# A 128x1 memset behind every indirect DMA, gathers four steps ahead, and silu one step later in an edge message-passing kernel

## The chip, the cores and the metric

The kernel runs on one core of a Trainium2 chip. The time is device microseconds for one execution of the program, the median of several runs. A profile is the record of one further execution on the same kind of core: its span goes from the first to the last recorded instruction. The engines are named as in the profile: PE (TensorE), ACT (ScalarE), DVE (VectorE), POOL (GpSimd) and SP (SyncE, which issues DMAs).

## The reference

The reference is one layer of message passing on a graph with N = 12,500 nodes of D = 64 features and E = 800,000 edges with 4 features each; H = 128.

```python
def reference(x, e_attr, src, dst, w1, b1, w2, b2):
    h_src = x[src]
    h_dst = x[dst]
    m_in = concatenate([h_src, h_dst, e_attr], axis=-1)
    h = silu(m_in @ w1 + b1)
    msg = h @ w2 + b2
    return segment_sum(msg, dst, N)
```

Since the sum over edges is linear, the kernel sums the hidden rows h of each node first, with a count of the edges, and multiplies the sums by w2 once per node at the end.

## The kernel before

**Tables.** At the start the products of x with the source part and with the target part of w1 are made for all nodes. The source product goes to the table `Atab` in device memory, one row of 512 bytes a node. The target product stays on chip as `Btab`.

**Sorting.** The edges come in no order. The kernel sorts them by target into 98 buckets of 128 nodes, in 16 portions. For each portion, `rank` counts the edges of each bucket, and `place` (line 879) moves the edges' records to their places: one-hot matmuls (L983) into a PSUM tile `pl`, a copy by ACT into `cb` (L958), and an indirect DMA of GpSimd that scatters the rows of `cb` into a buffer `buf` in device memory (L944). All but the first portion is sorted while edges of earlier portions are already worked on.

**The main loop.** `run` (line 1193) goes over 1590 steps of 512 sorted edges (4 tiles of 128). What step n needs is issued by small functions, each some steps ahead or behind (the constants of line 1187):

- `load` (SP, 11 steps ahead) and `pairs` (SP, 10 ahead) bring the edges' sources and targets, for two steps at once; `sources` (DVE, L1091, 8 ahead) turns them into row numbers `ix`.
- `gather` (GpSimd, 6 ahead) issues four indirect DMAs (L1155), each of 128 rows of `Atab`, into one of seven buffers `ga`.
- `spread` (SP, 4 ahead), `marks` (DVE, 1 ahead) and `targets` (ACT, L1118 and L1119, 2 ahead) prepare the edge features `pts`, the one-hot tiles `ob` of the sums, and the one-hot tiles `oT` of the targets.
- `pre` (PE, step n itself) sums edge features (L1143), target rows (L1145) and the gathered source rows (L1147) in a PSUM tile `px`. L1147 is the last reader of `ga`.
- `silu` (ACT, L1166, step n itself, right after `pre`) writes h from `px`. `onehot` (ACT, L1162) makes `sg` from `ob` one step later.
- `seg` (PE, L1174, two steps later) sums h by node into another tile of the same three PSUM buffers as `px`, and `accum` (DVE, L1182) adds that to the sums `S` in SBUF.

Between these stand pieces of `rank` and `place` for later portions. `filler` deals them out by estimated costs over the steps. Every engine executes its instructions in the order in which the code writes them (`in_order`, line 1047), so a waiting instruction holds up all that is written behind it on its engine. Two waits matter for the gathers: for `ix`, and for a `ga` buffer. With seven buffers and a lead of six, the gathers for step n+6 write the buffer of step n-1, which is free when L1147 of step n-1 is done.

After the loop the sums are transposed, multiplied by w2, and written out.

Of the kernel before, what the change touches and what calls it, by code (L numbers as in the profile page):

```python
# [11 lines left out]
BF = mybir.dt.bfloat16  # L12
# [69 lines left out]
def tile_mpnn(ctx, tc, x, e_attr, src, dst, w1, b1, w2, b2, out, portions):  # L82
# [8 lines left out]
    VE, SC, GP, PE = nc.vector, nc.scalar, nc.gpsimd, nc.tensor  # L91
# [728 lines left out]
    def records(p, c0, cn):  # L820
# [53 lines left out]
        p["rec", c0] = (pay, lo, hv)  # L874
        yield 1200

    below = [zero[:, :CS * PC], zero[:, :CS * PC]]

    def place(p):
# [20 lines left out]
        for c0 in range(0, cols, PW):  # L900
# [6 lines left out]
            for g in range(c0 // GT, -(-(c0 + cn) // GT)):  # L907
# [10 lines left out]
                for s0 in range(0, gt, SUB):  # L918
                    flush(pend, 1)
                    sn = min(SUB, gt - s0)  # L920
                    co = None
                    if s0 + sn == gt:

                        if s0 < 2 * SUB:
                            flush(pend, 0)
                        co = wk.tile([128, NLO], BF, name="co")
                        VE.tensor_scalar(co[:R], io3[:R], p["cin"][:R, g:g + 1], None, op0=OP.is_equal)
                        yield 229
                    mk = wk.tile([128, SUB, CS * PC], FH, name="mk")
                    VE.tensor_tensor(  # L930
                        mk[:EP, :sn].bitcast(I32).rearrange("p s (f j) -> p s f j", f=PC),
                        half_[:, s0:s0 + sn].unsqueeze(2).to_broadcast([EP, sn, PC, CS // 2]),
                        pay[:EP, go + s0:go + s0 + sn].rearrange("p s w t -> p s (w t)").bitcast(I32).unsqueeze(3)
                        .to_broadcast([EP, sn, PC, CS // 2]), op=OP.bitwise_and)
                    yield 430
                    oh = wk.tile([128, SUB, NLO], BF, name="oh")
                    VE.tensor_tensor(  # L937
                        oh[:EP, :sn].rearrange("p s (j t) -> p s j t", t=2),
                        io3[:EP].rearrange("p (j t) -> p j t", t=2).unsqueeze(1).to_broadcast([EP, sn, NLO // 2, 2]),
                        lo[:EP, go + s0:go + s0 + sn].unsqueeze(2).to_broadcast([EP, sn, NLO // 2, 2]), op=OP.is_equal)  # L940
                    yield 700

                    def scatter(ix_, n_, rows_):
                            stn = GP.indirect_dma_start(  # L944
                                out=buf, out_offset=bass.IndirectOffsetOnAxis(ap=ix_, axis=0),
                                in_=rows_, in_offset=None, bounds_check=NCH - 1, oob_is_err=False)
                            tc.add_to_no_dep_group(f"S{k}", stn.ins)
                            for kk in range(k + 1):
                                tc.declare_no_dep(stn.ins, group=f"S{kk}", reason="distinct rows")
                            for kk in range(k + 1, len(ports)):  # L950
                                tc.declare_no_dep(stn.ins, group=f"Z{kk}", reason="rows of later portions alone")
                            if k:
                                tc.declare_no_dep(stn.ins, group="L", reason="rows of an earlier portion")

                    def store(g, pa):
                        flush(scat, 2)
                        cb = wk.tile([128, NQ + 1, CS * PC], FH, name="cb", bufs=3)
                        SC.activation(cb.rearrange("p q c -> p (q c)"), pa, AF.Copy)  # L958
                        below[:] = cb[:, 1], cb[:, 2]
                        todo = [(p["idx"][:, g:g + 1], 128, cb[:, 0])]  # L960
                        if g + 1 == ngr:
                            todo.append((p["idx"][:, ngr:ngr + 1], 128, cb[:, 1]))
                            if k == last:
                                todo.append((p["fidx"][:R, 0:1], R, cb[:R, 2]))
                        for i, a in enumerate(todo):
                            defer(scat, lambda a=a: scatter(*a), 3 + i)


                    d, at = (1, 0) if clock["half"] else (0, 3)

                    def mm(g=g, s0=s0, mk=mk, oh=oh, gt=gt, sn=sn, co=co, at=at):
                        if s0 == 0:
                            box[0] = ps.tile([128, (NQ + 1) * CS * PC], F32, name="pl", bufs=2)
                        pa = box[0]
                        done_ = s0 + sn == gt
                        terms = [(oh[:EP, i], mk[:EP, i])
                                 for i in range(sn)]
                        if done_:
                            flush(evac, 0)
                            terms.append((co[:R], below[1][:R]))  # L980
                        for i, (oh_, mv) in enumerate(terms):
                            for u in range(3):
                                PE.matmul(pa[:, u * CS * PC:(u + 1) * CS * PC], oh_[:, u * 128:(u + 1) * 128], mv,  # L983
                                          start=s0 + i + u == 0, stop=False)
                        if done_:
                            PE.matmul(pa[:, :CS * PC], idb, below[0], start=False, stop=True)
                            defer(evac, lambda: store(g, pa), int(at == 3), 3 - at)
                    defer(pend, mm, d, at)
                    yield 229
                    subs -= 1  # L990
                    while nxt is not None:
                        c = next(nxt, None)
                        if c is None:
                            nxt = None
                            break
                        yield c
                        if subs > 0:
                            break
# [152 lines left out]
    def gather(n):  # L1151
        s = st[n]
        ga = wk.tile([128, 4, 2 * H], FH, name="ga", bufs=NGA)
        for t in range(4):
            GP.indirect_dma_start(out=ga[:, t, :], out_offset=None, in_=Atab,  # L1155
                                  in_offset=bass.IndirectOffsetOnAxis(ap=s["ix"][:, t:t + 1], axis=0))
        s["ga"] = ga

    def onehot(n):
# [24 lines left out]
            st.pop(n)  # L1184
            bts.pop(n)

    LL, LP, LX, LG, LS, LR, LT = 11, 10, 8, 6, 4, 1, 2
    phase = []
    for k, b in enumerate(sure):
        assert b > len(phase) + LL + 2  # L1190
# [2 lines left out]
    def run(m0, m1, filler):  # L1193

        bt = bt0 = None
        prev = {}
        ahead = m0
        for n in range(m0 - LL, m1 + 2):
            def on(lag):
                return m0 <= n + lag < m1  # L1200
            m = n + LL
            i0 = traced()
            clock["now"] = n
            if on(LL):
                k = phase[m] if m < len(phase) else len(ports) - 1
                filler(m, 0)
                if m % 64 == 0 or m == m0 or m < len(phase) and phase[m - 1] != k:
                    bt, bt0 = bucket_table(k, 2 * m), 2 * m
                bts[m] = (bt, 2 * m - bt0)
                if m == ahead:  # L1210
                    w = min(WL, m1 - m, len(phase) - m if m < len(phase) else WL)
                    w = 1 + sum(all(phase[m + j] == k for j in range(1, i + 1) if m + j < len(phase)) for i in range(1, w))
                    load(m, k, w)
                    ahead += w
            if on(LP):
                pairs(n + LP)
            if on(LX):
                sources(n + LX)
            if on(LG):
                gather(n + LG)  # L1220
            if on(LS):
                spread(n + LS)
            if on(LR):
                marks(n + LR)
            if on(LT):
                targets(n + LT)
            if on(-2):
                seg(n - 2)
            if on(-1):
                onehot(n - 1)  # L1230
            if on(0):
                pre(n)
                silu(n)
            at_place(0, n)
            at_place(1, n)
            for t in range(4):
                clock["half"] = int(t > 1)
                filler(n, 1 + t)
                if t == 1:
                    at_place(2, n)  # L1240
                if on(-2) and t == 3:
                    accum(n - 2, 0)
            filler(n, 5)
            if on(-2):
                accum(n - 2, 1)
            at_place(3, n)
            in_order(i0, prev)
        clock["now"] = None
        assert not any(places)
# [175 lines left out]
```

## Time and profile before

| | |
|---|---|
| median of 3 runs | 11,317.32 us (11,317.08 to 11,324.34) |
| span of the profiled execution | 11,179.7 us |
| instructions recorded | 214,957 |
| mean granted TensorE clock | 0.809 of full speed |
| first gather starts | 317.8 us |
| last gather starts | 11,106.5 us |

The page gives the span of the profiled execution and not its time from outside; the median of the runs lies 137.6 us above the span. Its rows are read thus: a group has line, engine, operation, output and input, shapes and number of instructions, then its busy time, the mean of one in ns, and the idle time of the engine right before these instructions with what ended most of it. "remote" and "issue" stand where no single instruction was found as the one that ended a wait: "issue" is time in which the engine waited for nothing that the profile shows. A row of the timeline has start, duration, engine, line, operation, and in brackets the idle time before it and what ended it.

### The profile page before, as it was taken

How to read it: one execution, taken by the hardware profiler on the slowest of the kernel's cores; microseconds unless marked ns; L12 is line 12 of the kernel's file. 1: busy time of each engine (PE TensorE's matmuls, PEld its weight loads, DVE VectorE, ACT ScalarE, POOL GpSimd, SP SyncE). 2: the span in 40 equal slices, each digit the busy share in tenths (PEclk: the TensorE clock that was granted, in tenths of full speed). 3: DMA queues.
4: the chain of work that ended last, by engine and by line, in shares of the span. 5: the costliest groups of instructions: out<-in, count | busy, mean ns of one | idle time of the engine just before them, and what ended most of it. 6: DMA issues, size and time to landing. Idle time of an engine off the chain costs nothing. (4 is left out here: it accounts for less than half of the span.)

```text
span 11179.7 us, 214957 instructions
## 1 busy us (share of the span) xinstructions
PE 8116.8 (73%) x73739; PEld 6653.7 (60%) x73739; DVE 6365.6 (57%) x18821; ACT 3859.6 (35%) x5331; POOL 6499.4 (58%) x6828
## 2 busy tenths in 40 slices
PE   7677777777777777777777777777777777775556
PEld 5566666666666566566566566666565565554445
DVE  8666676666665555555655555655555665441112
ACT  3233333333333333333333333333333333333333
POOL 1555555555555665566655666566566566666664
PEclk8777888888888778888888888888788887877777
DMA  2334434443443444444444444444444444444444
GB/s 92 64 66 72 67 58 71 65 73 64 72 66 64 76 67 66 76 68 67 77 66 66 76 68 66 74 69 68 75 67 66 74 67 69 69 67 71 72 72 68
DMA packets 3427360, 777.19 MB, mean 70 GB/s; under 512 B 3152950, under 2 KB 3215334, under 8 KB 3425036
## 3 DMA queue, kind: packets, MB, share of 16 engines
q1 hardware_dynamic: 3206638, 316.00, 26.1%
q0 software_dynamic: 218016, 446.07, 15.1%
q8 instruction: 645, 10.57, 0.4%
q14 instruction: 399, 3.27, 0.1%
q10 hardware_dynamic: 1662, 1.29, 0.0%
HBM read 712.51 MB, written 54.08 MB: 69 GB/s over the span
## 5 line engine op out<-in xcount | busy, mean ns | idle before, releaser
L1155 POOL DMA_INDIRECT ga<-Atab,ix x6360 | 6050.6, 951 | 4120.9 <-issue 1511.7
L1166 ACT ACTIVATE h<-px 128x512 f32<-128x512 f32 x1590 | 946.7, 595 | 6596.1 <-remote 2752.7
L1174 PE MATMUL px<-h,sg 128*128 128x129 f32 x12720 | 2375.2, 337 | 928.6 <-issue 387.7
L1174 PEld LDWEIGHTS px<-h,sg 128*128 128x128 f32 x12720 | 2065.8, 240 | 1155.0 <-issue 533.8
L983 PE MATMUL pl<-mk,oh 128*128 128x160 f16 x18750 | 1987.5, 260 | 575.8 <-issue 493.3
L983 PEld LDWEIGHTS <-oh 128*128 128x128 bf16 x18750 | 1637.8, 110 | 1037.3 <-issue 767.7
L1145 PE MATMUL px<-Btab,oT 128*128 x12720 | 1731.0, 249 | 159.4 <-issue 154.0
L1143 PE MATMUL px<-WE,pts 65*128 65x128 bf16 x6360 | 1489.0, 250 | 383.5 <-issue 241.1
L1182 DVE TENSOR_TENSOR S<-S,px 128x129 f32 x3180 | 906.2, 285 | 1341.2 <-remote 562.5
L1145 PEld LDWEIGHTS <-oT 128*128 128x128 bf16 x12720 | 1233.0, 114 | 575.1 <-issue 523.4
L930 DVE TENSOR_TENSOR mk<-fix,pay 128x320 int32<-128x320 int32 x1563 | 758.1, 485 | 1322.5 <-remote 712.0
L937 DVE TENSOR_TENSOR oh<-fix,lo 128x1536 bf16<-128x1536 bf16 x1563 | 1482.4, 948 | 0.1
L1147 PE MATMUL px<-ga,idA 128*128 128x512 f16 x3180 | 1172.0, 454 | 51.6 <-issue 46.2
L591 DVE TENSOR_REDUCE slT<-rx 128x5 f32<-128x490 f32 (+1 forms) x1302 | 833.2, 642 | 614.1 <-remote 305.1
L1119 ACT ACTIVATE oT<-oT,scl 128x1024 bf16<-128x1024 bf16 x795 | 986.1, 1240 | 26.7
L1162 ACT ACTIVATE sg<-ob 128x512 f32<-128x512 bf16 x1590 | 982.1, 618 | 0.0
L1118 ACT ACTIVATE oT<-oT,nip 128x1024 bf16<-128x1024 f16 x795 | 906.9, 1141 | 31.6 <-DMA oT<-dsc 24.7
L1143 PEld LDWEIGHTS <-pts 65*128 65x128 f16 x6360 | 722.2, 114 | 159.6 <-issue 113.1
L583 PEld LDWEIGHTS <-selB 99*128 99x128 bf16 x6250 | 479.1, 108 | 539.7 <-issue 428.3
L1128 DVE TENSOR_TENSOR ob<-fix,d 128x1024 bf16<-128x1024 bf16 x795 | 550.1, 692 | 352.3 <-ACT sg L1162 164.8
L583 PE MATMUL rx<-bT,selB 99*128 99x98 bf16 x6250 | 598.4, 224 | 198.1 <-issue 189.1
L579 PE MATMUL rx<-ohb,triO 128*128 128x490 bf16 (+1 forms) x1302 | 541.6, 416 | 120.5 <-DVE slT L591 49.8
(326 smaller groups left out, 5973.1 us busy)
## 6 DMA issues: line engine op xcount, KB each, us to landing
oT<-dsc SPq DMA_DIRECT2D x795, 256.0 KB
ga<-Atab,ix POOLq DMA_INDIRECT x6360
pts<-buf SPq DMA_DIRECT2D x2385, 16.0 KB
buf<-zero SPq DMA_DIRECT2D x184, 120.0 KB
dsc<-buf SPq DMA_DIRECT2D x795, 4.0 KB
pld<-dsc SPq DMA_DIRECT2D x795, 4.0 KB
Btab<-in_e_attr_dram POOLq DMA_DIRECT2D x10, 1250.0 KB
el<-in_e_attr_dram SPq DMA_DIRECT2D x74, 160.0 KB
```

Source lines behind the costliest of these rows:

```text
L583: PE.matmul(xp[:EP, i * R:(i + 1) * R], selB[:NR, s_:s_ + 1].to_broadcast([NR, EP]), bT[g][:NR, :R], start=False, stop=i == n - 1)
L937: VE.tensor_tensor(oh[:EP, :sn].rearrange("p s (j t) -> p s j t", t=2), io3[:EP].rearrange("p (j t) -> p j t", t=2).unsqueeze(1).to_broadc ...
L983: PE.matmul(pa[:, u * CS * PC:(u + 1) * CS * PC], oh_[:, u * 128:(u + 1) * 128], mv, start=s0 + i + u == 0, stop=False)
L1118: SC.activation(oT, oT.bitcast(FH), AF.Abs, bias=nip1[:, 0:1])
L1119: SC.activation(oT, oT, AF.Relu, scale=scl[:, 2:3], bias=inv)
L1143: PE.matmul(pr[:, sl], s["pts"][:, sl], WE, start=t == 0, stop=False)
L1145: PE.matmul(pr[:, sl], s["oT"][:, sl], Btab[:, ds(v[t // 2], 1), u, :], start=False, stop=False)
L1147: PE.matmul(pr.rearrange("p (t h) -> p t h", t=4), idA, s["ga"][:, :, u * H:(u + 1) * H], start=False, stop=u == 1)
L1155: GP.indirect_dma_start(out=ga[:, t, :], out_offset=None, in_=Atab, in_offset=bass.IndirectOffsetOnAxis(ap=s["ix"][:, t:t + 1], axis=0))
L1162: SC.activation(sg, s["ob"][:, :4].rearrange("p t h -> p (t h)"), AF.Copy)
L1166: SC.activation(hs[n % 3][:, :, :H], st[n]["pr"].rearrange("p (t h) -> p t h", t=4), AF.Silu)
L1174: PE.matmul(s["so"][t // 2], s["sg"][:, t * 128:(t + 1) * 128], hs[n % 3][:, t, :], start=t % 2 == 0, stop=t % 2 == 1)
```

## The change

The change has three parts. GpSimd clears a tile `idle` of 128x1 bf16, which nothing reads, behind each scatter and each gather. The loads, pairs, sources and gathers come two steps nearer to their use, the gathers four steps ahead in place of six; the other leads and the number of `ga` buffers stay. And `silu(n)` is issued early in step n+1, behind the loads and ahead of all else of that step, in place of step n right after `pre(n)`.

```diff
+    idle = cst.tile([128, 1], BF, name="idle")
     below = [zero[:, :CS * PC], zero[:, :CS * PC]]
...
                             stn = GP.indirect_dma_start(
                                 out=buf, out_offset=bass.IndirectOffsetOnAxis(ap=ix_, axis=0),
                                 in_=rows_, in_offset=None, bounds_check=NCH - 1, oob_is_err=False)
+                            GP.memset(idle, 0.0)
...
         for t in range(4):
             GP.indirect_dma_start(out=ga[:, t, :], out_offset=None, in_=Atab,
                                   in_offset=bass.IndirectOffsetOnAxis(ap=s["ix"][:, t:t + 1], axis=0))
+            GP.memset(idle, 0.0)
...
-    LL, LP, LX, LG, LS, LR, LT = 11, 10, 8, 6, 4, 1, 2
+    LL, LP, LX, LG, LS, LR, LT = 9, 8, 6, 4, 4, 1, 2
...
+            if on(-1):
+                silu(n - 1)
             if on(LP):
                 pairs(n + LP)
...
             if on(0):
                 pre(n)
-                silu(n)
             at_place(0, n)
```

Two places show the new order. The first is GpSimd's queue where the second portion's first scatter comes in, behind the gathers of the first thirty steps. Before (the number at the end says how often the row repeats):

```order
L373 MEMSET S 128x1806
L944 DMA buf<-cb,idx 76544x160 x8
L1155 DMA ga<-Atab,ix 128x256 x120
L944 DMA buf<-cb,idx 76544x160
L1155 DMA ga<-Atab,ix 128x256 x12
```

And after, from the last gather ahead of that scatter on (the lines have moved: L1157 is the gather, L945 the scatter, L948 and L1159 the memsets):

```order
L1157 DMA ga<-Atab,ix 128x256
L1159 MEMSET idle 128x1
L945 DMA buf<-cb,idx 76544x160
L948 MEMSET idle 128x1
L1157 DMA ga<-Atab,ix 128x256
L1159 MEMSET idle 128x1
L1157 DMA ga<-Atab,ix 128x256
L1159 MEMSET idle 128x1
```

Gathers and scatters keep their order among each other on this queue; a memset stands behind each.

The second place is ACT's queue in the middle of the loop, in a step that also copies a `pl` tile into `cb`. Before:

```order
L1162 ACTIVATE sg<-ob 128x512
L1166 ACTIVATE h_217<-px 128x4x128
L958 ACTIVATE cb<-pl 128x480
L1162 ACTIVATE sg<-ob 128x512
L1166 ACTIVATE h_219<-px 128x4x128
```

After (L1165 is the copy of `ob`, L960 that of `pl`, L1169 the silu):

```order
L1165 ACTIVATE sg<-ob 128x512
L960 ACTIVATE cb<-pl 128x480
L1169 ACTIVATE h_222<-px 128x4x128
L1165 ACTIVATE sg<-ob 128x512
L1169 ACTIVATE h_218<-px 128x4x128
```

The silu now stands behind the `cb` copy of its step instead of ahead of it; the three h buffers are named by number.

## The prediction

> **What bounds the kernel now.** I read the busy line of the page first, then the stretch from the first gather to the last one, because the share of the span averages a different prologue and epilogue.
>
> ```profile
> PE 8116.8 (73%) x73739; PEld 6653.7 (60%) x73739; DVE 6365.6 (57%) x18821; ACT 3859.6 (35%) x5331; POOL 6499.4 (58%) x6828
> L1155 POOL DMA_INDIRECT ga<-Atab,ix x6360: 942/947/1623, 317.8 to 11106.5; - x199
> 317.50:11108.00 10790.50, 7830.32 (x71293) 6424.31 (x71292) 6072.12 (x17925) 3741.82 (x5126) 6446.50 (x6749) 0.81 0.42 69
> ```
>
> The third row (columns: window, its length, busy time and instructions of PE, PEld, DVE, ACT and POOL, granted clock, DMA share, GB/s) holds the 1590 steps: 10,790.5 us, 6.79 us a step. No engine is full: TensorE 73%, GpSimd 60%. So the bound is a wait, and I ask who waits for whom. GpSimd's groups in that same stretch:
>
> ```profile
> L1155 POOL DMA_INDIRECT ga<-Atab,ix x6360 | 6050.6, 951 | 4120.9 <-issue 1511.7 <-remote 862.2 <-PE px L1147 759.5
> L944 POOL DMA_INDIRECT buf<-cb,idx x388 | 394.9, 1018 | 231.4 <-ACT cb L958 119.8 <-issue 111.0 <-ACT h L1166 0.6
> POOL ga L1155 <- issue: 1511.7, 4896, 4.9
> POOL buf L944 <- issue: 111.6, 366, 0.3
> POOL ga L1155 <- DVE ix L1091: 23.7, 7, 9.4
> ```
>
> It issues 6360 gathers and 389 scatters there. The two issue rows say that 4896 + 366 = 5262 of them start behind another indirect DMA, after a gap of 0.31 us in which nothing is waited for. The timeline shows the pitch, and how one step runs:
>
> ```profile
> 6014.84 0.95 POOL L1155 DMA_INDIRECT ga<-Atab,ix  x1 [1.37 <-remote]
> 6016.09 0.95 POOL L1155 DMA_INDIRECT ga<-Atab,ix  x1 [0.30 <-issue]
> 6016.56 0.59 PE L1147 MATMUL px<-ga,idA 128*128 128x512 f16 x2
> 6017.34 0.94 POOL L1155 DMA_INDIRECT ga<-Atab,ix  x1 [0.30 <-issue]
> 6018.59 0.95 POOL L1155 DMA_INDIRECT ga<-Atab,ix  x1 [0.31 <-issue]
> 6019.84 1.01 POOL L944 DMA_INDIRECT buf<-cb,idx  x1 [0.30 <-issue]
> 6022.04 0.60 ACT L1166 ACTIVATE h<-px 128x512 f32<-128x512 f32 x1 [6.32 <-remote]
> 6022.16 0.49 DVE L930 TENSOR_TENSOR mk<-fix,pay 128x320 int32<-128x320 int32 x1 [1.93 <-remote]
> 6022.27 0.97 POOL L1155 DMA_INDIRECT ga<-Atab,ix  x1 [1.42 <-remote]
> ```
>
> Start to start, a gather takes 1.25 us (6014.84 to 6016.09). Were GpSimd never held up, the stretch would need 6360 x 1.25 + 389 x 1.32 (1.01 + 0.31) = 7950 + 513 = 8463 us. It takes 10,790. The difference, **2327 us or 1.46 us a step**, is what waiting costs.
>
> What does it wait for? The last matmul on the px tile ends at 6017.15. The silu that reads that tile starts at 6022.04, 4.9 us later, and ACT was idle for 6.32 us. In that very moment DVE (6022.16) and GpSimd (6022.27) start as well, all 1.2 to 1.4 us after the last indirect DMA ended (6020.85). The release seems to come with the end of GpSimd's run of DMAs, not with the matmul. The tail, which has no sorting work beside it, shows the same behind a run of eight:
>
> ```profile
> 10400.30 0.95 POOL L1155 DMA_INDIRECT ga<-Atab,ix  x1 [2.09 <-PE px L1145]
> 10406.70 1.06 PE L1147 MATMUL px<-ga,idA 128*128 128x512 f16 x2
> 10409.05 0.94 POOL L1155 DMA_INDIRECT ga<-Atab,ix  x1 [0.30 <-issue]
> 10411.80 0.60 ACT L1166 ACTIVATE h<-px 128x512 f32<-128x512 f32 x1 [7.32 <-PE px L1147]
> 10411.90 0.61 DVE L1182 TENSOR_TENSOR S<-S,px 128x129 f32 x2 [5.33 <-PE px L1147]
> 10412.04 0.95 POOL L1155 DMA_INDIRECT ga<-Atab,ix  x1 [2.04 <-PE px L1147]
> ```
>
> The matmul ends at 10407.76, the silu starts 4.0 us later, 1.8 us behind the end of the run at 10409.99. Now a place where GpSimd had run out of work:
>
> ```profile
> 6032.19 0.95 POOL L1155 DMA_INDIRECT ga<-Atab,ix  x1 [0.30 <-issue]
> 6035.09 1.06 PE L1147 MATMUL px<-ga,idA 128*128 128x512 f16 x2
> 6036.18 0.60 ACT L1166 ACTIVATE h<-px 128x512 f32<-128x512 f32 x1 [6.40 <-PE px L1147]
> 6036.42 0.94 POOL L1155 DMA_INDIRECT ga<-Atab,ix  x1 [3.28 <-PE px L1147]
> ```
>
> GpSimd idle since 6033.14, the matmul ends at 6036.15, the silu starts 0.03 us later. I call it the **hold**: TensorE's progress reaches the others late while a run of indirect DMAs is in the air. GpSimd in turn waits for the buffer that the same step's matmul frees (seven ga buffers, gathers six steps ahead), so hold and buffer chase each other: run, hold, release, run. How the hold comes about the trace doesn't show.
>
> **The change, part by part.** *The memsets.* Behind each of the 6749 indirect DMAs of the stretch stands one more GpSimd instruction. Nothing reads the tile, and it waits for nobody but GpSimd itself. Rows that are near:
>
> ```profile
> 0.27 0.11 POOL L1409 MEMSET const-float32-1.0<- 128x1 f32 x1
> 0.30 0.12 POOL L1409 MEMSET const-bfloat16-1.0<- 128x1 bf16 x1
> 1.43 0.09 POOL L135 MEMSET ones_b<- 128x1 bf16 x1
> 176.87 0.98 POOL L944 DMA_INDIRECT buf<-cb,idx  x1 [3.72 <-ACT cb L958]
> 177.84 0.52 POOL L356 MEMSET sg<- 1x512 f32 x1
> ```
>
> The same tile shape took 0.09 us; two in a row started 0.03 us apart. Behind a scatter a memset started at once (176.87 + 0.98 against 177.84), without the 0.30 us that a DMA behind a DMA shows. Bounds: 0.03 us each when the start-to-start step is what counts, 0.03 x 6749 = 202 us; even a gain is not excluded if the 0.31 us gap shrinks, which I bound at 0.31 x 5262 = 1631 us and think unlikely. From above: 0.09 and a second gap of 0.31, 0.40 x 6749 = 2700 us. I take 0.10 us, by the row of the same shape: **+675 us**.
>
> [...] The memset at 177.84 shows no delay, but it is one. [...]
>
> What the memset does to the hold is the open term. The prologue's lone scatters have a memset behind them, but no matmul that somebody waits for ended in their shadow. From one side it does nothing (the hold hangs on the transfer); from the other it ends it (the hold hangs on GpSimd's program, and an ordinary instruction closes the DMA). The second is nearer to the rows: the waiters start together with the end of the run, however long the run is (five DMAs: 1.2 us after it; eight: 1.8 us), so each DMA that follows another keeps the hold up, and a non-DMA instruction between them breaks just this succession.
>
> *Gathers four steps ahead instead of six.* Seven ga buffers stay. Before, gather n+6 overwrites the buffer of step n-1, which TensorE has only just read; after, gather n+4 takes that of step n-3. The wait for the buffer goes: TensorE may be two steps further behind. What is late next: the data. Issue to use falls from six steps to four, some 24 us at 6 us a step, against a landing that the release rows put at under 2 us; free. load, pairs and sources move with the gather and keep their distance to it; SyncE issues the same DMAs in the same order. On GpSimd's queue gathers and scatters keep their order too, memsets apart.
>
> *silu a step later.* It goes behind the cb copy in some steps:
>
> ```profile
> L958 ACT ACTIVATE cb<-pl 128x480 f16<-128x480 f32 x391 | 221.6, 567 | 457.4 <-remote 264.8 <-PE pl L986 157.3 <-PE px L1147 16.1
> L1166 ACT ACTIVATE h<-px 128x512 f32<-128x512 f32 x1590 | 946.7, 595 | 6596.1 <-remote 2752.7 <-PE px L1147 1959.4 <-PE rx L583 578.0
> ```
>
> The copy need not wait behind a silu whose px is late any more; the silu waits at most one copy, 0.57 us, 391 times. Between 0 and 222 us lost, between 0 and the 120 us that scatters waited for the copy won. Cover: seg, the next reader, comes two steps behind pre, and ACT stands idle 6596 us in front of silus. No PSUM buffer comes free too late: the next to take the px of pre(n) is seg(n), which needs silu(n) anyway. I take 0.
>
> *The sum.* Waits of 2327 us go, except those for data of the step itself, 120 + 24 = 144 us, and half of GpSimd's named waits for L1147 (759.5 / 2 = 380 us), for the places where TensorE really is late, as at 6036.42. Stretch: 8463 + 675 + 144 + 380 = 9662 us. Around it 317.5 us before and 72 after: span 10,051 (before: 11,179.7). The median of the runs is 11,317.32, that is 137.6 us above the span; the same added gives 10,189. I forecast **10,190 us**.
>
> **Rivals.** *B, the hold stays, only the buffer wait goes.* Then GpSimd runs two steps at a stretch, as in the tail: 10400.30 to 10412.04 is 11.74 us for eight gathers, plus scatters 2 x 389/1590 x 1.32 = 0.65, plus 8.5 memsets 0.85: 13.24 per two steps, x 795 = 10,526, + 527 = 11,050 us. For it: the landing, which no memset changes, is what the release follows. Against: it needs the sorting's instructions, of which the tail has none, to fit between.
>
> *C, slower: the hold stays and longer runs starve the rest.* All engines' progress then comes once in two steps, and in the gap behind each run TensorE, ACT and DVE do two steps' dependent work. The tail's gap is 2.04 us; with the sorting's work it would be more, 3.28 us as at 6036.42: (13.24 + 1.24) x 795 + 527 = 12,040 us. It decides from a gap of 2.40 us on, where 13.60 x 795 + 527 = 11,339 passes the time of before.
>
> *D, nothing measurable,* 11,317 us: the memsets vanish in the issue gaps and the hold is as before, one run a step, because something else than the buffer paces GpSimd.
>
> *E, there is no hold.* TensorE's ends in the trace would be early and the silus start when the matmul is really done. Then the buffer wait was no loss by itself, and 5262 back-to-back DMAs grow by 0.10: 11,317 + 526 = 11,843 us. Against it: 0.03 us at 6036.18 and 4.9 us at 6022.04 behind the same line. [...]
>
> **Chances.** The hold ends, 10,190: 0.57 (its own range 9,200, the sum with 0.03 us memsets and no wait left, 8463 + 202 + 527, to 10,860, with 0.20 us memsets). B 0.15, D 0.06, C 0.13, E 0.09. Faster is A and B, 0.72; slower is C and E, 0.22; within 0.2%, about what a measurement of this kernel can tell from no change, D, 0.06. The range reaches from 9,200 to 11,700: below it lies 0.04 of A (memsets that cost less than nothing), above it E and about 0.07 of C, 0.2 together.
>
> **What would show it.** If the hold ends: silus start within 0.1 us of L1147's end while gathers run, ACT's wait before silu turns from remote to the matmul, and GpSimd's gathers follow at 1.3 to 1.4 us with few waits. The memset's price is the start-to-start step of two gathers with it between. If B or C: runs of eight, silus still at a run's end. If E: rows as before with a longer pitch. The forecast fails if the memset opens a second 0.3 us gap, or if TensorE, at 4.9 us of work a step, becomes the bound.

## The result, and the profile after

The changed kernel took 12,639.2 us (median of 4 runs), the kernel before 11,317.2 us on the same chip: **11.6% slower**, ratio 1.1159 with a 95% interval of 1.1143 to 1.1175. The forecast was 10,190 us with a range to 11,700; it had the wrong sign. The outcome is that of rival C, and worse than C was priced.

The page of the changed kernel and its groups (line, engine, operation, tiles, shapes and number; busy us and mean ns of one; idle time before them and what ended it). L1157 is the gather, L1159 the memset behind it, L1169 the silu:

```profile
span 12638.4 us, 222031 instructions
PE 8409.8 (67%) x73739; PEld 6842.4 (54%) x73739; DVE 6357.1 (50%) x18821; ACT 3845.2 (30%) x5331; POOL 7276.7 (58%) x13596
L1157 POOL DMA_INDIRECT ga<-Atab,ix x6360 | 6039.5, 950 | 4732.1 <-issue 2278.4 <-PE px L1177 460.4 <-PE px L1149 460.1
L1159 POOL MEMSET idle<- 128x1 bf16 x6360 | 760.8, 120 | 3.5
L1169 ACT ACTIVATE h<-px 128x512 f32<-128x512 f32 x1590 | 943.6, 593 | 6409.3 <-remote 3401.6 <-PE px L1149 1897.5 <-PE rx L583 387.7
POOL ga L1157 <- issue: 2278.4, 5599, 12.2
```

TensorE, DVE and ACT do the work of before, spread over 1459 us more. The idle time before silus that no single instruction ended grew from 2753 to 3402 us. And 5599 gathers now follow something else on GpSimd with no named wait between, against 4896 before: GpSimd's runs have become longer. Counted over the traces of the loop, where an idle time above 0.6 us ends a run, its indirect DMAs form 1023 runs against 1368, and 563 of them hold eight or nine against 217.

The timeline shows such a run, with GpSimd's DMAs and the other engines' rows around them:

```profile
6039.73 0.94 POOL L1157 DMA_INDIRECT ga<-Atab,ix  x1 [4.78 <-issue]
6040.67 0.12 POOL L1159 MEMSET idle<- 128x1 bf16 x1
6040.98 0.94 POOL L1157 DMA_INDIRECT ga<-Atab,ix  x1 [0.19 <-issue]
6041.98 0.60 ACT L1169 ACTIVATE h<-px 128x512 f32<-128x512 f32 x1 [1.67 <-PE px L1149]
6047.05 0.38 PE L1149 MATMUL px<-ga,idA 128*128 128x512 f16 x1 [0.34 <-issue]
6048.47 0.94 POOL L1157 DMA_INDIRECT ga<-Atab,ix  x1 [0.19 <-issue]
6051.36 0.67 DVE L591 TENSOR_REDUCE slT<-rx 128x5 f32<-128x490 f32 x1 [7.20 <-PE rx L583]
6051.62 0.60 ACT L1169 ACTIVATE h<-px 128x512 f32<-128x512 f32 x1 [8.53 <-PE rx L583]
6055.06 0.94 POOL L1157 DMA_INDIRECT ga<-Atab,ix  x1 [5.53 <-PE px L1177]
```

From 6039.73 to 6049.41 GpSimd sends eight gathers, two steps' worth, at the old pitch of 1.25 us. The memsets sit in the gap between two DMAs: 0.12 us of the 0.31. The matmul on px ends at 6047.43, and its silu starts 4.2 us later, 2.2 us behind the run's end. DVE and ACT have stood for 7.2 and 8.5 us. Only then do they and TensorE do what the next gathers need, and GpSimd waits 5.5 us for it. The windows of this run give the share of each engine (length; busy us and instructions of PE, PEld, DVE, ACT, POOL; clock, DMA share, GB/s):

```profile
6039.70:6044.70 5.00, 4.79 (x55) 4.19 (x53) 4.35 (x14) 1.72 (x4) 4.24 (x8) 0.91 0.41 52
6044.70:6050.70 6.00, 1.97 (x8) 0.72 (x9) 0.00 (x0) 0.00 (x0) 4.24 (x8) 0.73 0.31 55
6050.70:6055.70 5.00, 4.69 (x41) 4.35 (x41) 3.82 (x11) 3.84 (x5) 0.64 (x1) 0.65 0.39 62
```

In the first four gathers the others work off what had been released. In the second four DVE and ACT start no instruction, and TensorE 8 matmuls against 55. The second step's gathers thus run beside engines that do next to nothing, and in the 5 us after them it is GpSimd that idles.

### The profile page after: what moved, and what is told of

It reads as the page before. It is cut to its first block, busy times and chain, and to the rows that moved or that the text cites. A ratio compares the mean times of both kernels' runs of the same rounds, so it can differ in the third digit from the quotient of the medians.

```text
span 12638.4 us, 222031 instructions
## 1 busy us (share of the span) xinstructions
PE 8409.8 (67%) x73739; PEld 6842.4 (54%) x73739; DVE 6357.1 (50%) x18821; ACT 3845.2 (30%) x5331; POOL 7276.7 (58%) x13596
## 5 line engine op out<-in xcount | busy, mean ns | idle before, releaser
L1157 POOL DMA_INDIRECT ga<-Atab,ix x6360 | 6039.5, 950 | 4732.1 <-issue 2278.4
L1177 PE MATMUL px<-h,sg 128*128 128x129 f32 x12720 | 2417.3, 343 | 980.9 <-issue 470.5
L1169 ACT ACTIVATE h<-px 128x512 f32<-128x512 f32 x1590 | 943.6, 593 | 6409.3 <-remote 3401.6
L1177 PEld LDWEIGHTS px<-h,sg 128*128 128x128 f32 x12720 | 2125.5, 247 | 1181.2 <-issue 598.9
L985 PE MATMUL pl<-mk,oh 128*128 128x160 f16 x18750 | 2122.3, 266 | 945.6 <-issue 849.1
L985 PEld LDWEIGHTS <-oh 128*128 128x128 bf16 x18750 | 1693.1, 113 | 1497.5 <-issue 1236.7
L1147 PE MATMUL px<-Btab,oT 128*128 x12720 | 1763.6, 253 | 362.6 <-issue 351.3
L1145 PE MATMUL px<-WE,pts 65*128 65x128 bf16 x6360 | 1514.6, 254 | 728.6 <-ACT h L1169 415.6
L1149 PE MATMUL px<-ga,idA 128*128 128x512 f16 x3180 | 1217.9, 467 | 127.5 <-issue 111.0
L1165 ACT ACTIVATE sg<-ob 128x512 f32<-128x512 bf16 x1590 | 981.7, 617 | 0.0
L960 ACT ACTIVATE cb<-pl 128x480 f16<-128x480 f32 x391 | 221.5, 566 | 2120.3 <-PE pl L988 979.8
L1159 POOL MEMSET idle<- 128x1 bf16 x6360 | 760.8, 120 | 3.5
```

Source lines behind the costliest of these rows:

```text
L1145: PE.matmul(pr[:, sl], s["pts"][:, sl], WE, start=t == 0, stop=False)
L1147: PE.matmul(pr[:, sl], s["oT"][:, sl], Btab[:, ds(v[t // 2], 1), u, :], start=False, stop=False)
L1149: PE.matmul(pr.rearrange("p (t h) -> p t h", t=4), idA, s["ga"][:, :, u * H:(u + 1) * H], start=False, stop=u == 1)
L1165: SC.activation(sg, s["ob"][:, :4].rearrange("p t h -> p (t h)"), AF.Copy)
L1169: SC.activation(hs[n % 3][:, :, :H], st[n]["pr"].rearrange("p (t h) -> p t h", t=4), AF.Silu)
L1177: PE.matmul(s["so"][t // 2], s["sg"][:, t * 128:(t + 1) * 128], hs[n % 3][:, t, :], start=t % 2 == 0, stop=t % 2 == 1)
```

## The experiments

Three theories stood against each other: (1) more free buffers let GpSimd run two steps at a stretch, and the hold then covers both; (2) the memsets lengthen the hold; (3) the silu, now behind a copy that waits for a later matmul, comes too late. Each run was timed beside the kernel before on the same chip; ratios are to that.

### One part at a time

`e1_memset`: the memsets alone.

```diff
+    idle = cst.tile([128, 1], BF, name="idle")
...
                                in_=rows_, in_offset=None, bounds_check=NCH - 1, oob_is_err=False)
+                            GP.memset(idle, 0.0)
...
                                   in_offset=bass.IndirectOffsetOnAxis(ap=s["ix"][:, t:t + 1], axis=0))
+            GP.memset(idle, 0.0)
```

> The memsets alone; leads and silu as before. Theory 1 (runs of eight: the leads free the gathers of the buffer wait, GpSimd sends two steps at a stretch, and TensorE's progress reaches the others once in two steps): runs stay at four or five, and as the changed kernel's gathers still start 1.25 us apart with a memset between, the time stays within 1% of 11,317 us. Theory 2 (the memsets lengthen the hold or break into the release): slower by several per cent, toward 12,600 us, with runs of four and a longer idle time behind each. Theory 3 (the silu behind the copy of pl): 11,317 us as well.

`e2_leads`: the leads alone.

```diff
-    LL, LP, LX, LG, LS, LR, LT = 11, 10, 8, 6, 4, 1, 2
+    LL, LP, LX, LG, LS, LR, LT = 9, 8, 6, 4, 4, 1, 2
```

> The leads alone (9, 8, 6, 4), seven ga buffers, no memsets, silu as before. Theory 1: most of the loss is here, 12,200 to 12,700 us, runs of eight and nine gathers in the main stretch, silus late by most of a run. Theory 2: 11,317 us or faster, since a wait is gone and nothing is added. Theory 3: 11,317 us.

`e3_silu`: the silu alone.

```diff
+            if on(-1):
+                silu(n - 1)
             if on(LP):
...
                 pre(n)
-                silu(n)
```

> The silu one step later alone. Theory 1: within 1% of 11,317 us. Theory 2: the same. Theory 3 (in a step with a copy of pl the silu waits behind it, and the copy for a matmul that TensorE issues later than the px; 2120 us of idle time stand before these copies in the changed kernel, 457 before): 11,700 to 12,600 us, the idle time before the copies at about 2000 us and that of TensorE for h up.

`e4_leads_silu`: the last two diffs together.

> The changed kernel without its memsets. Theory 1 and theory 3: 12,639 us as the changed kernel, within 1%, since the memsets fit the gap between two indirect DMAs. Theory 2: near 11,317 us. If the memsets help against the hold after all, slower than 12,639 us.

| | us | before | ratio (95%) |
|---|---|---|---|
| memsets | 11,266.5 | 11,200.0 | 1.0058 (1.0041 to 1.0075) |
| leads | 12,254.3 | 11,200.0 | 1.0956 (1.0930 to 1.0982) |
| silu | 11,258.5 | 11,200.0 | 1.0052 (1.0035 to 1.0069) |
| leads and silu | 12,291.3 | 11,200.0 | 1.0980 (1.0953 to 1.1007) |

The leads carry the loss. The memsets do not end the hold. Their kernel's groups, and the gathers' own wait in the kernel with the leads alone:

```profile
L1157 POOL DMA_INDIRECT ga<-Atab,ix x6360 | 6056.5, 952 | 3438.7 <-issue 945.7 <-PE px L1149 927.2 <-remote 893.0
L1169 ACT ACTIVATE h<-px 128x512 f32<-128x512 f32 x1590 | 946.5, 595 | 6681.1 <-remote 2819.0 <-PE px L1149 2094.2 <-PE rx L583 629.9
POOL ga L1157 <- issue: 945.7, 4918, 5.1
```

```profile
POOL ga L1155 <- issue: 2807.9, 5526, 12.2
```

With memsets alone (first fence) GpSimd's waits for TensorE are not shorter (927 us by name and 893 unnamed, against 760 and 862 before), the silus' unnamed wait is 2819 us (2753 before), and 4918 gathers follow another instruction directly (4896 before). With the leads (second fence) it is 5526, near the changed kernel's 5599. The silu's half a per cent shows as idle time before the copies into `cb`, here in the silu-only kernel:

```profile
L958 ACT ACTIVATE cb<-pl 128x480 f16<-128x480 f32 x391 | 221.6, 567 | 1660.3 <-PE pl L986 691.5 <-remote 526.3 <-PE rx L583 179.7
```

It is 1660 us against 457, most of it idle time that stood before the silus otherwise (5475 us in place of 6596). So theory 3 has its mechanism, at a small price.

### Buffers, not the lead

`e7_nga5_leads` shortens the leads and takes two buffers away:

```diff
-NGA = 7
+NGA = 5
...
-    LL, LP, LX, LG, LS, LR, LT = 11, 10, 8, 6, 4, 1, 2
+    LL, LP, LX, LG, LS, LR, LT = 9, 8, 6, 4, 4, 1, 2
```

> The leads alone as in the run of that name, with five ga buffers in place of seven, so that the gathers of step n+4 write the buffer of step n-1 again. Theory 1 (the slack in buffers lets GpSimd run two steps at a stretch): runs of four and five are back and the time is within 1% of before, 11,200 us on the chip of the last runs, ratio 0.99 to 1.01. Rival (a lead of four steps is too short: gathered rows or row numbers come late): at least as slow as the leads alone, ratio 1.09 or more, since fewer buffers only add waits.

`e8_nga9` keeps the leads of before and adds two buffers:

```diff
-NGA = 7
+NGA = 9
```

> The kernel before with nine ga buffers in place of seven, leads as before: gathers of step n+6 write the buffer of step n-3. Theory 1: runs of eight and nine, ratio 1.07 to 1.11, as with the leads alone, though nothing is left out and nothing is late by its lead. Rival (the lead): no change, 0.995 to 1.005, or a gain since a wait is gone.

`e11_lead5` goes half the way with seven buffers:

```diff
-    LL, LP, LX, LG, LS, LR, LT = 11, 10, 8, 6, 4, 1, 2
+    LL, LP, LX, LG, LS, LR, LT = 10, 9, 7, 5, 4, 1, 2
```

> Half the step: load, pairs, sources and gather one step nearer (10, 9, 7, 5), seven ga buffers, so gathers of step n+5 write the buffer of step n-2. Theory 1: between before and the leads alone, ratio 1.03 to 1.08, with more runs of eight than before (its main stretch had 79 of eight beside 666 of four). Rival (the lead): no change until the lead is too short, ratio 0.99 to 1.02.

| | overwrites the buffer of | us | before | ratio (95%) |
|---|---|---|---|---|
| lead 4, five buffers | step n-1 | 11,177.4 | 11,182.9 | 0.9994 (0.9985 to 1.0004) |
| lead 5, seven buffers | step n-2 | 11,280.4 | 11,182.9 | 1.0092 (1.0075 to 1.0109) |
| lead 6, nine buffers | step n-3 | 12,234.7 | 11,182.9 | 1.0946 (1.0925 to 1.0967) |

The waits of the gathers in these three kernels, in the table's order:

```profile
POOL ga L1155 <- issue: 1514.8, 4907, 4.4
```

```profile
POOL ga L1155 <- issue: 1565.4, 4973, 6.8
```

```profile
POOL ga L1155 <- issue: 2799.7, 5514, 11.7
```

This settles it for the chips of these runs. A lead of four steps costs nothing by itself, and two more buffers with the old leads cost 9.5%. The wait for the buffer of step n-1 was a pacer: it kept GpSimd, in most runs, to one step (1127 of the 1368 runs of before have four or five DMAs). The half-way kernel was expected at 1.03 to 1.08 and came out at 1.009: with one more free buffer most runs stay at one step (4973 gathers directly behind another instruction), with two more they don't (5514). Why the second step joins only then was not tried.

### A break in place of the wait

`e10_pause` has the leads of the change, no short memsets, and one long one behind the fourth gather of each step.

```diff
+    idle = cst.tile([128, 1800], BF, name="idle")
...
         for t in range(4):
             GP.indirect_dma_start(out=ga[:, t, :], out_offset=None, in_=Atab,
                                   in_offset=bass.IndirectOffsetOnAxis(ap=s["ix"][:, t:t + 1], axis=0))
+        GP.memset(idle, 0.0)
```

> The leads alone, seven ga buffers, with one memset of 128x1800 bf16 (about 1.6 us by the 65x1024 rows of 0.95 us) behind the fourth gather of each step, none elsewhere. If what releases the others is the end of a run of DMAs plus the landing, whatever ends the run: silus start 1.1 to 1.3 us into the memset, GpSimd's pace is 5.0 + 1.6 + 0.3 a step, and the ratio is 0.98 to 1.03. If a short break does not matter and only GpSimd's waiting for TensorE paces the engines: ratio 1.08 to 1.2, as the leads alone and slower by the memsets.

It took 11,287.8 us, ratio 1.0090 (1.0073 to 1.0106). A break of 1.62 + 0.16 us, made here by a memset and not by a wait, undoes nearly all of the loss of the leads. The silus' wait is now a named one:

```profile
L1156 POOL DMA_INDIRECT ga<-Atab,ix x6360 | 6069.7, 954 | 1798.9 <-issue 1673.1 <-PE px L1148 18.7 <-DVE d L1127 14.2
L1168 ACT ACTIVATE h<-px 128x512 f32<-128x512 f32 x1590 | 948.6, 597 | 6527.3 <-PE px L1148 5218.9 <-issue 383.6 <-remote 244.9
```

GpSimd waits for nobody (19 us for px) and is itself the limit. The silus were expected within the break; the timeline shows one of them elsewhere:

```profile
6002.90 1.62 POOL L1158 MEMSET idle<- 128x1800 bf16 x1
6004.68 0.95 POOL L1156 DMA_INDIRECT ga<-Atab,ix  x1 [0.16 <-issue]
6005.93 0.94 POOL L1156 DMA_INDIRECT ga<-Atab,ix  x1 [0.30 <-issue]
6005.50 1.01 PE L1148 MATMUL px<-ga,idA 128*128 128x512 f16 x2 [4.85 <-DMA ga<-Atab,ix]
6006.55 0.60 ACT L1168 ACTIVATE h<-px 128x512 f32<-128x512 f32 x1 [5.76 <-PE px L1148]
```

It starts 1.9 us into the next run, 0.04 us after L1148 ends at 6006.51. What TensorE ends early in a run still gets through: counted over this trace, in 739 of the 1590 steps the last L1148 ends in the first 1 us of a run, and 96% of the silus of these steps start within 0.2 us of it. A shorter break should then have beaten the kernel before. Three lengths were tried, with the kernel of leads and short memsets beside them: 1430, 1100 and 750 columns in place of 1800 for `e12_pause13`, `e13_pause10` and `e14_pause07`; `e5_memset_leads` is the changed kernel with the silu in its old place.

> As the run with the pause, with 128x1430 bf16 behind the fourth gather: about 1.29 us plus 0.16 us until the next gather, 1.45 us between runs in place of 1.78. If GpSimd's own pace was the bound there (5.0 + 1.78 + scatters 0.33 a step, 1590 steps, is 11,300 us with 390 us around), this is 0.33 us a step or 525 us faster: ratio 0.96 to 0.98. If the engines need the 1.4 us that GpSimd idles in before (median behind a run of four), about the same gain; if the pause must outlast the hold by more than that, ratio 1.0 or above and waits for px back before the gathers.

> The pause at 128x1100 bf16, 0.99 + 0.16 = 1.15 us between runs. By GpSimd's pace alone 1000 us faster than the run with 1.78 us, ratio 0.91 to 0.93. If the others are released only 1.1 to 1.3 us after a run's last DMA (as ACT and DVE starts in the traces so far), most releases fall into the next run: its pace is no longer kept, GpSimd waits for buffers again and the ratio is 1.02 to 1.09.

> The pause at 128x750 bf16, 0.68 + 0.16 = 0.84 us between runs. If a release needs 1.1 us without a DMA after the last one, this pause does nothing and the ratio is that of the leads alone or worse, 1.08 to 1.12. By GpSimd's pace alone 0.88 to 0.90.

> Leads and short memsets, silu as before. The memsets cost 0.6% alone, the leads 9.6%, the silu 0.5% alone, the changed kernel 11.6%, leads and silu 9.8%. If the memsets cost more where runs are of eight (they would then stretch the hold), ratio 1.11 to 1.12; if the last 1.6% come from silu and memsets together, 1.095 to 1.105.

| | us | before | ratio (95%) |
|---|---|---|---|
| break of 1.45 us | 10,766.4 | 8,967.3 | 1.2006 (1.1986 to 1.2026) |
| break of 1.15 us | 10,333.4 | 8,967.3 | 1.1523 (1.1504 to 1.1543) |
| break of 0.84 us | 9,885.8 | 8,967.3 | 1.1024 (1.1006 to 1.1043) |
| leads and memsets | 8,973.8 | 8,967.3 | 1.0008 (0.9998 to 1.0018) |

The breaks are named by the lengths expected; the traces show 1.47, 1.19 and 0.90 us between runs.

No theory had expected this: on this chip the **kernel before** took 8967 us, 20% less than on the others. The breaks are a pure loss here, and the leads and memsets cost nothing.

### The other kind of chip

The changed kernel and the three breaks were run once more, to see whether it is the hold that differs.

> The changed kernel once more, beside the kernel before on the same chip. The chip of the last four runs took 8967 us for the kernel before, the others 11,183 to 11,317. If what differs is the hold (none on that chip: its silus waited for the matmul by name and GpSimd ran without a break), then on a chip where the kernel before takes about 11,200 us the ratio is 1.11 to 1.12 again with runs of eight, and on one where it takes about 8970 us it is 1.00 to 1.01, since GpSimd is full with either kernel and leads, memsets and silu move nothing.

> The pause of 1.15 us between runs once more. With the hold: ratio 0.91 to 0.95 if a release gets through in such a pause (10,333 us stood on the chip without the hold, GpSimd's own pace), 1.02 to 1.09 if it doesn't. Without the hold: 1.15 as measured.

> The pause of 1.45 us once more. With the hold: 0.96 to 0.98 if a release gets through in such a pause (10,766 us without the hold), near 1.0 or above if not. Without the hold: 1.20 as measured.

> The pause of 0.84 us once more. With the hold: 1.05 to 1.12 if a release needs more than that without a DMA, 0.88 to 0.95 if not. Without the hold: 1.10 as measured.

These four met another chip of the quick kind (the kernel before at 8974.1 us). The changed kernel took 8984.4 us, **ratio 1.0010 (1.0001 to 1.0020)**; the breaks of 1.15, 1.45 and 0.84 us came to 1.153, 1.201 and 1.103, as on the first. The changed kernel's trace there:

```profile
L1157 POOL DMA_INDIRECT ga<-Atab,ix x6360 | 6048.1, 951 | 1250.8 <-issue 1100.4 <-PE px L1149 21.2 <-PE px L1177 19.5
L1169 ACT ACTIVATE h<-px 128x512 f32<-128x512 f32 x1590 | 945.8, 595 | 3527.0 <-PE px L1149 3513.2 <-PE px L1147 7.0 <-issue 6.3
L1149 PE MATMUL px<-ga,idA 128*128 128x512 f16 x3180 | 1047.6, 414 | 1502.6 <-DMA ga<-Atab,ix 1438.2 <-issue 62.1
6001.56 0.97 POOL L1157 DMA_INDIRECT ga<-Atab,ix  x1 [0.18 <-issue]
6002.68 0.59 PE L1149 MATMUL px<-ga,idA 128*128 128x512 f16 x2 [1.73 <-DMA ga<-Atab,ix]
6002.83 0.94 POOL L1157 DMA_INDIRECT ga<-Atab,ix  x1 [0.19 <-issue]
6003.31 0.60 ACT L1169 ACTIVATE h<-px 128x512 f32<-128x512 f32 x1 [2.63 <-PE px L1149]
6004.08 1.05 POOL L1157 DMA_INDIRECT ga<-Atab,ix  x1 [0.19 <-issue]
```

There is no hold. The matmul ends at 6003.27 in the middle of GpSimd's run, and the silu starts 0.04 us later. The 3402 us of unnamed waits are gone; 3513 of 3527 us are for L1149 by name. GpSimd runs on at 1.25 us with 41 us of waits for px, and TensorE waits 1438 us for gathered rows. The bound is GpSimd, whose pitch the change leaves alone.

A slower GpSimd or ACT does not explain the difference between the chips: in the traces of the changed kernel a gather takes 950 and 951 ns on the two kinds, a silu 593 and 595 ns. The granted TensorE clock is lower where the hold is (0.76 against 0.89), but it does not make the hold: with the break of 1.45 us the quick chip granted 0.83, near the 0.81 of the kernel before elsewhere, and 6096 of the 6103 us before its silus are waits for the matmul by name.

Two more runs:

> The kernel before itself, for its trace on whichever kind of chip it meets. On one where it takes about 8970 us: silus start within 0.1 us of the last matmul on their px while gathers run, GpSimd's idle time is issue alone, and TensorE waits for gathered rows before L1147. On one where it takes about 11,200 us: as in the trace of before, which then only shows that the hold is the same on another chip.

> The pause of 1.15 us again. With the hold: ratio 0.91 to 0.95 if a release gets through in such a pause, 1.02 to 1.09 if not. Without the hold: 1.153, and nothing new.

They met a chip with the hold: the kernel before took 11,346.0 us, and 11,343.6 beside it, ratio 1.0004 (0.9993 to 1.0016). The break of 1.15 us took 11,833.3 us, **1.0429 (1.0397 to 1.0462)**. Its gathers' group, to be read beside that of the 1.78 us break:

```profile
L1156 POOL DMA_INDIRECT ga<-Atab,ix x6360 | 6050.3, 951 | 3128.7 <-issue 2111.7 <-PE px L1148 278.3 <-PE px L1176 154.2
```

The waits for px are back (278 us against 19). On these two chips with the hold, 1.15 us were too short for the releases, and 1.78 us passed them, at the price of GpSimd's own time. That fits the trace of before, in which the silus that start between two runs do so 1.24 us (median) after the run's last DMA. The same kernel shows both kinds of chip side by side: of the silus whose matmul ended during a run, 96% started within 0.1 us of it on the quick chip of the first 1.15 us run and 12% on this one. What lies between was measured only where no hold is. No kernel here beat the kernel before: lead four with five buffers equals it.

## Why the prediction was wrong

**The reading of the bound was right where it was taken.** The copy of the kernel before shows the hold again on another chip (3070 us of unnamed waits before its silus), and on the quick chips the same kernel takes 8967 us, against the sum of 8463 + 317.5 + 72 = 8853 us for a GpSimd that never waits. That term was off by 1.3%; the kernel before was not traced there, so that it has no hold on them is taken from the traces of the others. But the text took the hold for a property of the kernel; it is one of the kernel on some chips. The trace of one chip cannot show that.

**The step that failed first: "a non-DMA instruction between them breaks just this succession".** The memset doesn't end the hold. Alone it gave 1.0058 and shortened none of the waits for TensorE. The rows bore out only that many releases follow a run's end (1331 of the 1590 silus of before start between two runs); that any instruction would end a run was argued, not shown. A break of 1.78 us let the releases through on one chip with the hold (19 us of waits for px); one of 1.15 us didn't on another (278 us).

**The step that turned the sign: the buffer wait "goes", and its removal is "free".** The wait was priced as a loss of its own, with the data's lateness as the only thing to come behind it. It was the pacer. Without it most of GpSimd's DMAs go out in runs of two steps, and as the others get little done in the second half of such a run (the windows above), that half lies beside idle engines. That was rival C, given 0.13, because the page's waits were read as GpSimd's loss without asking whom GpSimd's idling served.

**C was priced too low, at 12,040 us.** Its term was the gap behind a run of eight, taken as 3.28 us from the nearest row. Three gaps of the changed kernel's timeline are 4.59 us (at 6023.34), 4.78 and 5.53; the mean behind its runs of eight and nine is 4.98 us. Five us in C's formula, without the memsets' 0.85, give (11.74 - 2.04 + 5.0 + 0.65) x 795 + 527 = 12,730 us if all steps ran in pairs; measured were 12,639. Not all did (379 runs of four or five stand beside the 563), so that it comes this close is in part luck.

**The memsets' price, 675 us: near nothing.** Each took 0.12 us (0.10 assumed), but inside the 0.31 us gap; the pitch stayed 1.25 us. Alone they cost 66 us on a chip with the hold; on a quick chip, where GpSimd is the bound, they and the leads together cost 6 us, with an interval that reaches zero. The bound "even a gain is not excluded" was not met either. A mean of 120 ns over 6360 of them in the changed kernel, with 3.5 us of idle time in all ahead of them, shows no delay of the memsets. On top of leads and silu the memsets cost more than alone (1.1159 against 1.0980); these two ratios were not measured side by side, and why is open.

**silu at 0: right to half a per cent.** It cost 0.52% alone (0.35 to 0.69), or 58 us, within the 222 us that bounded its loss. The bound itself left something out: it took the silu to wait for a copy's 0.57 us, but the copy now waits for a later matmul in front of it (1660 us of idle time against 457). Beside the leads it added no more than the two intervals allow.

**Rival E, no hold.** It was right of the chips without the hold, where a silu starts 0.04 us behind its matmul in the middle of a run; of the others it was not (4.2 us in the timeline above). Its chance of 0.09 was the author's estimate. In the trace of before, of 1226 silus whose matmul ended during a run 27 started within 0.1 us of it, and the median is 3.35 us.

**The 137.6 us outside the span were not outside.** The changed kernel's profiled run, one of its four timed ones, took 12,640.3 us with a span of 12,638.4. The profile of before is thus of another execution than its timed runs, 1.2% quicker. Chips with the hold differ by that much (11,183 to 11,344 us); on which chip it was taken is not on record.

## What to carry to other kernels

A wait that goes away has to be asked what it paced: when a producer's work holds up its consumers (here TensorE's progress shows late while GpSimd issues DMAs, 3.35 us late in the median of the trace of before; by what path is open), a tight ring of buffers can be what keeps it from starving them, and more buffers or slack then cost time. Before a change relies on such a wait going away, remove the wait alone, by as many more buffers at the old lead as the change would free: here one more free buffer cost 0.9%, two cost 9.5%. And where a kernel rests on such a balance, time it on several chips: the same change cost 11.6% on one and 0.1% on another.

## What the runs showed of the hardware that was not expected

- The kernel before took 8967 and 8974 us on two chips and 11,183, 11,200 and 11,344 us on three others (11,317 in the first comparison), each time steady within 0.3%. What the traces show to differ is the hold: on the first two a silu starts 0.04 us (median) behind its matmul during a run of indirect DMAs; in the two traces of the kernel before with the hold it starts 3.35 us (median) behind it, and mostly only once the run has ended. What makes a chip the one or the other is open.
- With the hold, TensorE itself issues slower late in a long run: 55 matmuls in the first 5 us of a run of eight gathers, 8 in the next 6 us, where the gaps stand as issue (1.11, 1.04, 0.76 us), not as waits. Over the changed kernel's 406 runs of eight or nine in the first 10,000 us it starts 9.8, 9.2, 3.0 and 1.2 matmuls a us in the first four stretches of 2.5 us; how much of that is want of work was not separated.
- A memset of 128x1 between two indirect DMAs of GpSimd costs no pitch: 1.25 us with and without it.
